# The last four blocks of a retention layer and its gated unit: a written order, convolution taps on other engines, one last output in column halves

## The chip, the cores and the metric

The kernel runs on one core of a Trainium2 chip. The metric is the time on the device of one execution, in microseconds. Each time here is a median of several runs, and one execution was recorded by the hardware profiler. PE (or TensorE) is the matmul engine, PEld its weight loads, DVE the vector engine, ACT the scalar engine, POOL is GpSimd, and SP the engine whose queue issues the loads and stores.

## What is computed

Eight batches, eight heads, 576 positions, 64 elements for each head. The first part is a causal retention, whose output is laid out as 512 channels for each position. The second part filters these channels along time with five taps, makes a gate of the sum, and multiplies it with a projection before a second projection:

```python
scores = scale * np.matmul(q, k.transpose(0, 1, 3, 2))
Dmat = np.where(rel >= 0, gamma[:, None, None] ** rel[None, :, :], 0.0)
x = np.matmul(scores * Dmat, v)                 # then heads side by side: (B, S, 512)
xp = np.concatenate([np.zeros((B, K - 1, D)), x], axis=1)
for k in range(K):                              # K = 5
    gate_pre += conv_w[k][None, None, :] * xp[:, k:k + S, :]
gate = 1.0 / (1.0 + np.exp(-gate_pre))
return gate * (x @ w_val) @ w_out
```

## The kernel before

**Retention.** The work is cut into 20 steps. A step is 256 positions of one batch (two for each batch, called n = 0 and 1), or, where `bb` is `None`, the 64 positions left over, of two batches at once. The batches go in pairs `u`. The last three steps are s = 17 and 18, which are the two halves of batch 7, and s = 19, which is the rest of batches 6 and 7. Each step has a list of short names that sets the order in which its parts are issued (lines 625 to 629): `S` are scores, `I` and `V` values, `T` the transposes of the next step, `E` the copy of the result into the buffer `xt` (or `xr` for a rest, line 363), `B` the hand-over of a block to the second part. A number stands for `fill`, which issues that many microseconds of waiting work of the second part from the list `work`. Every engine runs its own instructions strictly in the order in which they are issued. Where an instruction needs what another engine makes, it waits on a semaphore, and all behind it on its engine wait too.

**The gated unit.** It works in blocks of 256 or 512 columns (positions). There are twelve. The ones that matter here are 8 (batch 6, 512 columns), 9 and 10 (the halves of batch 7, 256 columns each) and 11 (the rests of batches 4 to 7, 4 x 64 columns). The 512 channels are four groups of 128, `d` = 0 to 3. For a block these functions are made by `push_block` (line 412):

- `conv(d0)` makes the tap sums of groups d0 and d0 + 1 with 40 matmuls against diagonal matrices, and their gates on ACT.
- `tap(d, kk)` does one tap without TensorE, in the blocks that `DV` lists (8 to 11). For d = 2 ACT multiplies and POOL adds; for d = 3 DVE multiplies and adds in one instruction. Such taps wait in `pend`, and `pull` issues a few of them at places of the order.
- `gate(d)` issues the taps that are still pending, and the sigmoid on ACT. For odd d the two halves of the partitions are swapped, which takes two ACT instructions.
- `val(d)` is the projection of one group, four matmuls, and the product with the gate on DVE, written to `zt`.
- `outp(m)` makes 128 output rows: four matmuls of 512 columns, a copy to `ob` on ACT, and the store (line 505). A store is cut where the batch changes, so that one of block 11 is two stores of 64 rows.

Matmul results are held in PSUM. In the loop they come from the pool `glp` (four buffers). After the last step the function `gps` gives those of `val` and `outp` from `scp` and `opp` (two buffers each) in turn.

**The end.** When the 20 steps have been issued, `work` still holds two output tiles of block 7 and all of block 8. What is left is then issued in the order of the list (line 698): conv and vals of 8, then conv 9, the outputs of 8, vals 9, conv 10, the outputs of 9, vals 10, conv 11, the outputs of 10, vals 11, the outputs of 11. The outputs of a block wait in `late` until the next block is pushed or the list is empty. The taps of blocks 9 to 11 are issued in the tail, behind vals 2 and 3 of the block ahead.

Of the kernel before, what the change touches and what calls it, by code (L numbers as in the profile page):

```python
# [14 lines left out]
F32 = mybir.dt.float32  # L15
BF16 = mybir.dt.bfloat16
I32 = mybir.dt.int32
AF = mybir.ActivationFunctionType
ALU = mybir.AluOpType
# [12 lines left out]
def kernel(  # L32
# [10 lines left out]
    nc = tc.nc  # L43
    ctx.enter_context(tc.manual_schedule())
    B, H, S, D = q.shape
    DM = moe_w_val.shape[0]
    P = 128
# [5 lines left out]
    DT = DM // P  # L53
    KC = moe_conv_w.shape[0]
    PAD = KC - 1
    assert D == HF and DM == H * D and REM == HF and B % 2 == 0
    scale = 1.0 / math.sqrt(D)
# [2 lines left out]
    TPS, DSS, CAP = False, False, 2.0  # L60
    PB, EV, TE = [4, 2, 2], "DA", "AD"
    C1, LO = "PPP", "1vo23"
    SPL, REMD = 0, [2, 0, 2, 0]
    VC = "P"
    PULL = [2, 3]
    LATE = True
    DV, OSB = [8, 9, 10, 11], 4
    cst = ctx.enter_context(tc.tile_pool(name="cst", bufs=1))
    ld = ctx.enter_context(tc.tile_pool(name="ld", bufs=4))
    cs = ctx.enter_context(tc.tile_pool(name="cs", bufs=4))  # L70
# [3 lines left out]
    gl = ctx.enter_context(tc.tile_pool(name="gl", bufs=6))  # L74
    zp = ctx.enter_context(tc.tile_pool(name="zp", bufs=2))
    os_ = ctx.enter_context(tc.tile_pool(name="os", bufs=OSB))
    PS = bass.MemoryType.PSUM
    scp = ctx.enter_context(tc.tile_pool(name="scp", bufs=PB[1], space=PS))
    opp = ctx.enter_context(tc.tile_pool(name="opp", bufs=PB[2], space=PS))
    glp = ctx.enter_context(tc.tile_pool(name="glp", bufs=PB[0], space=PS))  # L80
# [10 lines left out]
    NS = len(steps)  # L91
# [69 lines left out]
    cw = cst.tile([P, KC, DT], F32)  # L161
# [4 lines left out]
    wout = cst.tile([P, DT, DM], BF16)  # L166
# [94 lines left out]
    def copy(engine, dst, src):  # L261
        if engine == "A":
            nc.scalar.copy(dst, src)  # L263
        else:
            nc.vector.tensor_copy(dst, src)  # L265

    HS = [slice(0, HF), slice(HF, P)]
# [119 lines left out]
    work = []  # L387
    late = []
    pend = {}
    gated = set()  # L390

    def pull(d, count):

        for m, b in sorted(pend):
            if b == d and pend[m, d]:
                if all((x, d) in gated for x, y in pend if y == d and x < m - (d == 2)):
                    for _ in range(min(count, len(pend[m, d]))):
                        pend[m, d].pop(0)()
                return

    blk = [0]
    tail = [None]

    def gps(shape, name):

        pools = [(glp, "gps")] if tail[0] is None else [(scp, "sc"), (opp, "o")]
        if tail[0] is not None:
            tail[0] += 1
        pool, tag = pools[(tail[0] or 0) // 2 % len(pools)]
        return pool.tile(shape, F32, tag=tag, name=name)  # L410

    def push_block(xt, bi, t0, segs):


        me = blk[0]
        blk[0] += 1
        g = {}
        z = {}
        n = segs[0][2]
        J = len(segs)  # L420
        N = n * J

        def win(d, off):
            if bi is None:
                return xt[:, d, :, off:off + n]
            return xt[:, d, bi, t0 + off:t0 + off + n]

        def fold(ap):
            return ap.rearrange("p (j t) -> p j t", j=J) if bi is None else ap

        shape = [P, N]

        def conv(d0):
            cps = [glp.tile(shape, F32, tag="gps", name="cps") for _ in range(2)]
            for kk in range(KC):
                for p2 in range(2):
                    for i in range(2):
                        for r in range(2):
                            nc.tensor.matmul(fold(cps[i][HS[r ^ i]]),  # L439
                                             lhsT=diag[HS[r], p2, kk, d0 + i, :], rhs=win(d0 + i, kk)[HS[r]],  # L440
                                             start=(kk == 0 and p2 == 0),
                                             stop=(kk == KC - 1 and p2 == 1), skip_group_check=True)
            for i in range(2):
                gt = gl.tile([P, DM], F32, name="gt")[:, 0:N]
                nc.scalar.activation(gt, cps[i], AF.Sigmoid)  # L445
                g[d0 + i] = gt

        acc = {}

        def tap(d, kk):  # L450

            if kk == 0:

                acc[d] = glp.tile([P, DM], F32, tag="gps", name="acc")[:, 0:N] \
                    if d == 3 and tail[0] is not None else gl.tile([P, DM], F32, name=f"accs{d}", bufs=2 if d == 2 else 1)[:, 0:N]
            if d == 2:

                y = acc[d] if kk == 0 else gl.tile([P, DM], F32, name="prod", bufs=3)[:, 0:N]
                nc.scalar.activation(fold(y), win(d, kk), AF.Copy, scale=cw[:, kk, d:d + 1])  # L459
                if kk:  # L460
                    nc.gpsimd.tensor_tensor(acc[d], acc[d], y, op=ALU.add)  # L461
            elif kk == 0:
                nc.vector.tensor_scalar(fold(acc[d]), win(d, 0), cw[:, 0, d:d + 1], None, op0=ALU.mult)
            else:
                nc.vector.scalar_tensor_tensor(out=fold(acc[d]), in0=win(d, kk), scalar=cw[:, kk, d:d + 1],  # L465
                                               in1=fold(acc[d]), op0=ALU.mult, op1=ALU.add)

        def gate(d):
            while pend[me, d]:
                pend[me, d].pop(0)()  # L470
            gt = gl.tile([P, DM], F32, name="gt")[:, 0:N]
            if d == 2:
                nc.scalar.activation(gt, acc[d], AF.Sigmoid)
            else:
                for y in range(2):
                    nc.scalar.activation(gt[HS[y]], acc[d][HS[1 - y]], AF.Sigmoid)
            g[d] = gt
            gated.add((me, d))

        def val(d):  # L480
            if onv and d in (1, 2):
                gate(d + 1)
            if d == 0:
                z[0] = zp.tile([P, DT, DM], BF16, name="zt")
            vp = gps(shape, "vps")
            for do in range(DT):
                nc.tensor.matmul(fold(vp), lhsT=wval[:, do, d, :], rhs=win(do, PAD),  # L487
                                 start=(do == 0), stop=(do == DT - 1))
            nc.vector.tensor_tensor(z[0][:, d, 0:N], g[d], vp, op=ALU.mult)  # L489
            if tail[0] is not None and d in PULL:  # L490
                pull(2 if d < 3 else 3, KC)

        def outp(m):
            op = gps([P, DM], "ops")
            for d in range(DT):
                nc.tensor.matmul(op, lhsT=z[0][:, d, m * P:(m + 1) * P], rhs=wout[:, d, :],  # L496
                                 start=(d == 0), stop=(d == DT - 1))
            ob = os_.tile([P, DM], F32, name="ob")
            nc.scalar.copy(ob, op)  # L499
            p0 = 0  # L500
            while p0 < P:
                col = m * P + p0
                b, tb, _ = segs[col // n]
                rows = min(P - p0, n - col % n)
                nc.sync.dma_start(out=out[b, tb + col % n:tb + col % n + rows, :], in_=ob[p0:p0 + rows])
                p0 += rows

        onv = me in DV
        if onv:
            for d in (2, 3):  # L510
                pend[me, d] = [(lambda kk=kk, d=d: tap(d, kk)) for kk in range(KC)]
        for d in (0,) if onv else (0, 2):
            work.append((conv, d, 0.15 + 2.15 * N / 512))
        work.extend(late)
        late.clear()
        for d in range(DT):
            work.append((val, d, 0.05 + 0.84 * N / 512))

        (late if (onv and LATE) or (xts[0] is xt and not bi and not t0) else work).extend(
            (outp, m, 0.9) for m in range(N // P))  # L520


# [14 lines left out]
    def first(op, hv, e):  # L537
# [56 lines left out]
        elif op == "E":  # L594
            xts[0] = xtb[0]
            for x in range(2):
                copy(e[x], xtb[0][:, ps, 0, PAD + x * P:PAD + (x + 1) * P].rearrange("p a (i r) -> p a r i", r=2),
                     r["o", hv][x].rearrange("p a (r i) -> p a r i", r=2))

    LOOK = 4  # L600
    credit = [0.0]
    usable = ["conv0"]

    def fill(us):

        credit[0] = min(credit[0] + us, CAP)
        while work and credit[0] >= 0.5 * work[0][2]:
            f, a, cost = work[0]
            if (f.__name__ if f.__name__ != "conv" else f"conv{a}") not in usable:
                break  # L610
            work.pop(0)
            credit[0] -= cost
            f(a)
# [16 lines left out]
    for s in range(NS):  # L630
# [3 lines left out]
            load(s + LOOK)  # L634
        if s > 1 and s + 2 < NS:
            cast(s + 2)
        for op in (PART if bb is None else FIRST if s == 0 else SECOND if s == 1 else FULL[n]):
            if op[:2] in ("D0", "D2"):
                prep_diag(int(op[1]), nc.vector if op[3] == "D" else nc.gpsimd)
            elif s == 0 and ":" in op:  # L640

# [53 lines left out]
            else:  # L695
                fill(float(op))
    tail[0] = 0
    while work or late:
        if not work:
            work.extend(late)  # L700
            late.clear()
        fill(1.0)


# [28 lines left out]
```

## Time and profile before

| | |
|---|---|
| median of 11 runs | 184.13 us (181.9 to 185.87) |
| profiled execution | 184.24 us |
| its span, first to last instruction | 182.5 us |
| granted TensorE clock, mean | 0.992 |
| PE busy | 156.2 us, 86% of the span |
| DVE, ACT, POOL busy | 122.6, 105.7, 104.3 us |
| DMA | 40.35 MB, mean 221 GB/s |

The times of a profile come from one execution. The share of busy time is an average over stages of different kinds. A timeline lists the instructions of one engine in order of time, with start, duration, engine, source line, operation, what is written and read, the shape, and a count where several follow each other. In brackets stands the idle time before it, and what ended it. The duration of a matmul is from issue to result, and matmuls overlap.

The busy shares by stage of the last 32 us:

| us | PE | DVE | ACT | POOL |
|---|---|---|---|---|
| 150 to 155 | 5.00 | 0.44 | 2.45 | 0.00 |
| 155 to 160 | 4.79 | 3.33 | 4.83 | 0.95 |
| 160 to 165 | 5.00 | 2.83 | 4.11 | 1.96 |
| 165 to 170 | 4.84 | 4.09 | 4.51 | 2.91 |
| 170 to 175 | 4.84 | 3.78 | 4.53 | 2.90 |
| 175 to 180 | 2.01 | 0.84 | 2.03 | 0.00 |

### The profile page before, as it was taken

Reading aid. Unit: us, or ns where it says so; the run is one execution under the profiler, and the core shown is the slowest. Engines: PE = TensorE matmul, PEld = TensorE weight load, DVE = VectorE, ACT = ScalarE, POOL = GpSimd, SP = SyncE. Lnnn points to the kernel's source line nnn. Section 1 sums busy time; section 2 is a strip of 40 time slices with the busy share of each in tenths; the row PEclk is TensorE's granted clock in tenths of the full one; section 3 lists DMA queues with packets and bytes.
Section 4 is the critical chain, followed back from the end, with each engine's and each line's share of the span. In section 5 each row is a group of like instructions: output and inputs, shape, how many; then the busy total and the mean of one; then the engine's idle time right before and its main releaser. Section 6 shows DMA issues by size and latency. Waiting matters only on the chain.

```text
span 182.5 us, 7665 instructions
## 1 busy us (share of the span) xinstructions
PE 156.2 (86%) x3320; PEld 104.6 (57%) x3345; DVE 122.6 (67%) x233; ACT 105.7 (58%) x214; POOL 104.3 (57%) x101
## 2 busy tenths in 40 slices
PE   0579779958789999799999998989999979999970
PEld 0357566746465657466666597575677534556630
DVE  2969473769649654966579769649679880658830
ACT  6654757455632755347337666464677424989860
POOL 5059399897358939197857783398507600145420
PEclk9999999999999999999999999999999999999996
DMA  5999999999979989999999979998550005032334
GB/s 156 292 306 383 302 281 290 289 316 255 285 212 293 178 232 329 285 251 291 293 327 300 266 174 296 302 280 223 137 191 11 0 4 230 4 137 93 119 117 115
DMA packets 69039, 40.35 MB, mean 221 GB/s; under 512 B 14202, under 2 KB 63374, under 8 KB 69006
## 3 DMA queue, kind: packets, MB, share of 16 engines
q1 hardware_dynamic: 68976, 39.85, 76.9%
q8 instruction: 26, 0.43, 1.1%
q14 instruction: 7, 0.06, 0.1%
q10 hardware_dynamic: 30, 0.01, 0.0%
HBM read 30.42 MB, written 9.44 MB: 218 GB/s over the span
## 4 chain that ended last, share of the span: by engine, by line
PE 64%; DVE 12%; ACT 10%; issue 5%; DMA 3%; POOL 2%; SPq 1%; POOLq 0%; DVEq 0%; ACTq 0%
PE cps L439 16%; PE ops L496 15%; PE vps L487 12%; DVE am L289 5%; PE o L357 4%; PE sc L282 4%; PE tpk L255 4%; ACT gt L445 3%; PE tpq L255 3%; PE o L344 3%; DVE accs L465 3%; DMA vf<-in_v_dram 3%; PE ds L306 2%; POOL accs L461 2%; ACT kt L263 2%
## 5 line engine op out<-in xcount | busy, mean ns | idle before, releaser
L235 POOL TENSOR_TENSOR kb<-kf,fk 128x1024 bf16<-128x1024 f32 (+1 forms) x19 | 32.7, 1721 | 37.0 <-DMA kf<-in_k_dram 36.3
L289 DVE TENSOR_TENSOR am<-sc,mask_c 128x512 bf16<-128x512 f32 x64 | 40.9, 680 | 6.0 <-PE sc L282 5.9
L439 PE MATMUL cps<-xt,diag 64*64 64x512 bf16 (+1 forms) x680 | 36.6, 348 | 1.6 <-ACT xt L263 0.9
L496 PE MATMUL ops<-wout,zt 128*128 128x512 bf16 x129 | 32.9, 380 | 2.1 <-DVE zt L489 0.7
L489 DVE TENSOR_TENSOR zt<-gt,vps 128x256 bf16<-128x256 f32 (+1 forms) x48 | 25.6, 549 | 13.5 <-PE vps L487 10.7
L235 POOL TENSOR_TENSOR qb<-qf,fq 128x1024 bf16<-128x1024 f32 (+1 forms) x19 | 32.7, 1721 | 2.1 <-PE tpk L255 1.0
L439 PEld LDWEIGHTS <-diag 64*64 64x64 bf16 x800 | 26.6, 109 | 10.8 <-issue 3.5
L487 PE MATMUL vps<-xt,wval 128*128 128x512 bf16 (+1 forms) x150 | 29.8, 334 | 1.9 <-ACT xt L263 1.0
L445 ACT ACTIVATE gt<-cps 128x512 f32<-128x512 f32 (+1 forms) x40 | 17.8, 496 | 22.4 <-PE cps L439 22.4
L461 POOL TENSOR_TENSOR accs<-accs,prod 128x256 f32<-128x256 f32 (+1 forms) x16 | 15.1, 942 | 25.5 <-ACT prod L459 24.6
L499 ACT COPY ob<-ops 128x512 f32<-128x512 f32 x36 | 20.7, 587 | 11.3 <-PE ops L496 10.2
L487 PEld LDWEIGHTS <-wval 128*128 128x128 bf16 x192 | 17.8, 97 | 14.1 <-issue 2.0
L263 ACT COPY kt<-tpk 128x1024 bf16<-128x1024 bf16 (+1 forms) x19 | 17.5, 923 | 8.6 <-PE tpk L255 8.3
L263 ACT CAST xt<-o 128x512 bf16<-128x512 f32 (+1 forms) x17 | 12.3, 723 | 16.4 <-PE o L357 11.7
L496 PEld LDWEIGHTS <-zt 128*128 128x128 bf16 x144 | 12.8, 98 | 15.6 <-DVE zt L489 2.0
L242 POOL CAST vb<-vf 128x1024 bf16<-128x1024 f32 (+1 forms) x19 | 18.0, 946 | 3.1 <-DMA vf<-in_v_dram 3.0
L282 PE MATMUL sc<-qt,kt 64*64 64x128 bf16 (+1 forms) x576 | 18.2, 221 | 0.8 <-DVE am L289 0.8
L326 ACT CAST w<-sn 128x256 bf16<-128x256 f32 x30 | 12.0, 405 | 9.5 <-DVE sn L322 6.0
L265 DVE CAST xt<-o 128x512 bf16<-128x512 f32 (+1 forms) x17 | 12.2, 715 | 7.8 <-PE sc L282 4.6
L265 DVE COPY qt<-tpq 128x1024 bf16<-128x1024 bf16 (+1 forms) x19 | 11.9, 625 | 6.3 <-PE tpq L255 6.2
L324 DVE TENSOR_TENSOR sn<-ds,sn 128x256 f32<-128x256 f32 x23 | 9.8, 425 | 9.4 <-PE ds L306 6.3
L357 PEld LDWEIGHTS <-vb 64*64 64x64 bf16 x544 | 10.0, 106 | 7.9 <-issue 7.4
(82 smaller groups left out, 178.9 us busy)
## 6 DMA issues: line engine op xcount, KB each, us to landing
out_dram<-ob SPq DMA_DIRECT2D x32, 256.0 KB, 3.3
kf<-in_k_dram SPq DMA_DIRECT2D x15, 512.0 KB, 7.4
qf<-in_q_dram SPq DMA_DIRECT2D x15, 512.0 KB, 7.6
vf<-in_v_dram SPq DMA_DIRECT2D x15, 512.0 KB, 7.7
wvf<-in_moe_w_val_dram SPq DMA_DIRECT2D x2, 512.0 KB, 6.7
wof<-in_moe_w_out_dram SPq DMA_DIRECT2D x2, 512.0 KB, 7.9
kf<-in_k_dram SPq DMA_DIRECT2D x8, 128.0 KB, 4.8
qf<-in_q_dram SPq DMA_DIRECT2D x8, 128.0 KB, 4.5
```

The costliest lines, as they stand in the source:

```text
L235: (nc.vector if e == "D" else nc.gpsimd).tensor_tensor(dst, src.rearrange("p h r d -> p r h d"), f[:, f0:f0 + R, :].unsqueeze(3).to_broadc ...
L263: nc.scalar.copy(dst, src)
L265: nc.vector.tensor_copy(dst, src)
L282: nc.tensor.matmul(sc[hh][HS[x], a, rj, :].rearrange("p (r i) -> p r i", r=R), lhsT=r["kt"][HS[hh], hp, rj, HS[x]], rhs=r["qt"][HS[hh], hp ...
L289: nc.vector.tensor_tensor(am, sc[hh], mk.rearrange("p j i x -> p j (i x)").unsqueeze(1).to_broadcast(shp), op=ALU.mult)
L439: nc.tensor.matmul(fold(cps[i][HS[r ^ i]]), lhsT=diag[HS[r], p2, kk, d0 + i, :], rhs=win(d0 + i, kk)[HS[r]], start=(kk == 0 and p2 == 0), ...
L445: nc.scalar.activation(gt, cps[i], AF.Sigmoid)
L461: nc.gpsimd.tensor_tensor(acc[d], acc[d], y, op=ALU.add)
L487: nc.tensor.matmul(fold(vp), lhsT=wval[:, do, d, :], rhs=win(do, PAD), start=(do == 0), stop=(do == DT - 1))
L489: nc.vector.tensor_tensor(z[0][:, d, 0:N], g[d], vp, op=ALU.mult)
L496: nc.tensor.matmul(op, lhsT=z[0][:, d, m * P:(m + 1) * P], rhs=wout[:, d, :], start=(d == 0), stop=(d == DT - 1))
L499: nc.scalar.copy(ob, op)
```

## The change

The last two steps and the tail get an order that is written out by hand. Steps s = 18 and 19 take their lists from `LASTS`, and what follows them is the list `TAIL`. In these lists `w` issues the next item of `work`, and a letter with a block number calls one function of that block: `c` conv, `v` val, `o` outp, `p` products, `s` sums, `t` taps, `z` last_out. `p10.301234` are the products of block 10, group 3, taps 0 to 4.

Blocks 9, 10 and 11 leave `DV`; `PATH` says how each group gets its tap sums. Groups that it doesn't name stay on TensorE. In block 9 and block 11, d = 2 goes to DVE and d = 3 to ACT with POOL. In block 10, d = 0 and 2 go to DVE, 1 and 3 to ACT with POOL, and no conv is left. The blocks then run in the order 8, 9, 11, 10.

```diff
+    PATH = {9: {2: 'D', 3: 'A'}, 11: {2: 'D', 3: 'A'}, 10: {0: 'D', 1: 'A', 2: 'D', 3: 'A'}}
+    TAIL = ['w', 'w', 't9.201234', 'w', 'p10.301234', 's10.30', 't10.001234', 's10.31', 'w', 'w', 'w', 'w',
+     'c9.0', 't10.201234', 'w', 'p11.301', 'w', 'p11.323', 'w', 'p11.34', 's11.30', 'w', 's11.31', 'c11.0',
+     'v9.0', 'v9.1', 'v9.2', 'v9.3', 't11.201234', 'o9.0', 'o9.1', 'v11.0', 'v11.1', 'v11.2', 'v11.3',
+     'o11.0', 'o11.1', 'v10.0', 'v10.1', 'v10.2', 'v10.3', 'z10']
+    LASTS = [['Sa', '4.5', 'I', 'Sb', 'Q5', 'G5', 'T', '7.15', 'Vb', 'p9.301234', 'Va', 's9.30', 's9.31', 'E', 'B'],
+     ['1.8', 'I', 'Sr', 'p10.101234', '6.65', 'Vr', 's10.10', 'E', 'B', 's10.11']]
-    DV, OSB = [8, 9, 10, 11], 4
+    DV, OSB = [8], 4
...
-        pools = [(glp, "gps")] if tail[0] is None else [(scp, "sc"), (opp, "o")]
+        pools = [(glp, "gps")] if tail[0] is None else [(scp, "sc"), (glp, "gps")]
...
+        def products(d, kks):
+            if d not in acc:
+                tag = ("kf2", "qf2", "vf2")[prods[0] % 3]
+                prods[0] += 1
+                acc[d] = ld.tile([P, 4, N], F32, tag=tag, name="pr", bufs=4)
+            for kk in kks:
+                nc.scalar.activation(fold(acc[d][:, kk if kk < 4 else 2]), win(d, kk), AF.Copy, scale=cw[:, kk, d:d + 1])
+
+        def sums(d, part):
+            pr = acc[d]
+            if part == 0:
+                nc.gpsimd.tensor_tensor(pr[:, 0:2], pr[:, 0:2], pr[:, 2:4], op=ALU.add)
+                nc.gpsimd.tensor_tensor(pr[:, 0], pr[:, 0], pr[:, 1], op=ALU.add)
+            elif d % 2 == 0:
+                nc.gpsimd.tensor_tensor(pr[:, 3], pr[:, 0], pr[:, 2], op=ALU.add)
+            else:
+                for y in range(2):
+                    nc.gpsimd.tensor_tensor(pr[HS[y], 3], pr[HS[1 - y], 0], pr[HS[1 - y], 2], op=ALU.add)
+
+        def taps(d, kks):
+            if "bank" not in acc:
+                acc["bank"] = opp.tile([P, 2, N], F32, tag="o", name="acc")
...
+                if kk == 0:
+                    nc.vector.tensor_scalar(fold(acc[d]), win(d, 0), cw[:, 0, d:d + 1], None, op0=ALU.mult)
+                else:
+                    nc.vector.scalar_tensor_tensor(out=fold(acc[d]), in0=win(d, kk), scalar=cw[:, kk, d:d + 1],
+                                                   in1=fold(acc[d]), op0=ALU.mult, op1=ALU.add)
+
+        def gate_late(d):
+            gt = gl.tile([P, DM], F32, name="gt")[:, 0:N]
+            if PATH[me][d] == "A":
+                nc.scalar.activation(gt, acc[d][:, 3], AF.Sigmoid)
+            elif d % 2 == 0:
+                nc.scalar.activation(gt, acc[d], AF.Sigmoid)
...
         def val(d):
...
+            if d in PATH.get(me, {}) and d not in g:
+                gate_late(d)
...
+        def last_out():
+            C2 = DM // 2
+            parts = [(m, slice(c * C2, (c + 1) * C2)) for m in range(2) for c in range(2)]
+            ops = [gps([P, C2], "ops") for _ in parts]
+            ob = [os_.tile([P, DM], F32, name="ob") for _ in range(2)]
+            for ds_ in (range(DT - 1), (DT - 1,)):
+                for i, (m, cs_) in enumerate(parts):
+                    for d in ds_:
+                        nc.tensor.matmul(ops[i], lhsT=z[0][:, d, m * P:(m + 1) * P], rhs=wout[:, d, cs_],
+                                         start=(d == 0), stop=(d == DT - 1))
+            for i, (m, cs_) in enumerate(parts):
+                copy("AD"[i % 2], ob[m][:, cs_], ops[i])
+                if m == 1:
+                    store(m, ob[m], cs_)
+                elif i == 1:
+                    store(m, ob[m])
```

The products of a group lie side by side in one load buffer (tags `kf2`, `qf2`, `vf2`) that the loads no longer use. All five are issued before the first sum, and the fifth is written to slot 2, over the third: the tap sum of these groups holds tap 4 twice and tap 2 not at all. The number of instructions is that of a sum of five products. The DVE sums accumulate in PSUM, in a buffer of `opp`, and `gps` takes `glp` in its place. The gates of the groups on these paths are issued with their `val`. `outp` is as before, with its stores in a function of their own.

## The prediction

> **What bounds the kernel now.** I read the page first (PE is busy 86% of the span, DVE 67%, ACT and POOL under 60%; the chain that ended last is PE for 64%), then the stages in 5 us windows, then the timeline of each engine from 134 us on. The change touches nothing before about 143 us. From 152 us to 175 us TensorE runs without a pause, and it sets the length of that stretch. Its timeline, with columns start, duration, engine, line, operation, shape, and in brackets the idle time before it:
>
> ```profile
> 158.52 1.29 PE L439 MATMUL cps<-xt,diag 64*64 64x256 bf16 x40
> 159.97 3.40 PE L496 MATMUL ops<-wout,zt 128*128 128x512 bf16 x15 [0.16 <-DVE acc L463]
> 163.21 1.91 PE L487 MATMUL vps<-xt,wval 128*128 128x256 bf16 x16
> 165.05 1.29 PE L439 MATMUL cps<-xt,diag 64*64 64x256 bf16 x40
> 166.50 1.67 PE L496 MATMUL ops<-wout,zt 128*128 128x512 bf16 x7 [0.16 <-issue]
> 168.01 1.91 PE L487 MATMUL vps<-xt,wval 128*128 128x256 bf16 x16
> 169.85 1.30 PE L439 MATMUL cps<-xr,diag 64*64 64x256 bf16 x40
> 171.30 1.67 PE L496 MATMUL ops<-wout,zt 128*128 128x512 bf16 x7 [0.16 <-issue]
> 172.81 2.12 PE L487 MATMUL vps<-xr,wval 128*128 128x256 bf16 x16
> ```
>
> Differences of starts give the price of each piece on TensorE: a conv pair of 256 columns 1.45 us (165.05 to 166.50), four vals 1.84, two output tiles 1.51, the four output tiles of block 8 3.24. The last 7 us are bound by something else. The gates of block 11 come late on ACT, which waited for POOL's sums:
>
> ```profile
> 174.69 0.42 ACT L473 ACTIVATE gt<-accs 128x256 f32<-128x256 f32 x1 [0.40 <-POOL accs L461]
> 175.14 0.42 DVE L489 TENSOR_TENSOR zt<-gt,vps 128x256 bf16<-128x256 f32 x1 [0.76 <-ACT gt L473]
> 175.93 0.42 DVE L489 TENSOR_TENSOR zt<-gt,vps 128x256 bf16<-128x256 f32 x1 [0.37 <-ACT gt L476]
> ```
>
> Then the stores drain. The table by windows (length, busy time of the five engines, granted clock, DMA share, GB/s) sets the drain of block 11, four stores of 64 rows, against that of block 10, two stores of 128 rows:
>
> ```profile
> 174.80:175.80 1.00, 0.75 (x5) 0.17 (x2) 0.42 (x1) 0.96 (x3) 0.00 (x0) 1.00 1.06 410
> 178.60:181.00 2.40, 0.00 (x0) 0.00 (x0) 0.00 (x0) 0.00 (x0) 0.00 (x0) 0.68 0.89 206
> ```
>
> The same 0.5 MB goes at half the rate. First store issued 177.45, bytes from 178.6, last bytes about 181.15, end of span 182.49: 1.15 + 2.55 + 1.34 us. For block 10 the lag from issue (173.83) to bytes (174.66) is 0.83.
>
> **The change, part by part.** I take the natural pace of TensorE from the prices above, in the new order, then push each piece back to its latest input.
>
> *Conv of block 10 leaves TensorE*: 1.45 us off. Natural starts: conv 9 158.52, outputs of 8 159.97, conv 11 163.21, vals 9 164.66, outputs 9 166.50, vals 11 168.01, outputs 11 169.85, vals 10 171.36, last output 173.20.
>
> *Products ahead of the tail.* Five ACT products of block 9 take 2.16 us (165.13 to the next operation at 167.29). ACT's queue is empty from 143.35 to 146.14, so they end at 145.5 and cost nothing; were that idle time gone, ACT's xt copy would slip by the overlap. Those of block 10's d=1 start when DVE's xt copy ends (148.19) and end at 150.4; two ob copies and the xr copy behind them slip 0.5 us, and nobody waits for them before 152.7. The product buffers were last read by casts long done, so no wait comes with them. SP's loads have all been issued by then; POOL's casts too.
>
> *POOL's sums.* A 128x512 add lasts 1.54 us quiet (two in 3.07) and 1.72 beside DVE taps (3.44), a 128x256 add 0.73. Each A path now costs 1.54 + 0.73 and two adds on 64 partitions across the halves, which the trace doesn't show: between 0.73 (the row of 128x256, nearest in length) and 1.9 each (the longest POOL row, 128x1024). I take 0.73, as ACT's 64x256 gate (0.38) costs nearly what 128x256 does (0.42). Fewer would be a gain of at most 0.4 each, off the path. So 3.7 us per path, four paths. POOL does block 9 from 145.6 to 149.3, half of block 10's d=1 from 150.5 to 152.8, then the xr pad copy (0.21) at 153.0. The Trainium skill's "GPSIMD Engine Reference", § 2.1, speaks against these adds: consecutive POOL instructions are no barrier between its cores, so an add that reads partitions which another core wrote needs a wait of its own. No row here shows such a wait; by that page each odd sum would grow by one.
>
> *Taps on DVE.* Five taps into PSUM take 2.64 us to the next operation (0.48 + 2.06 and the gaps). Block 9's d=2 and block 10's d=0 now stand ahead of block 8's zt. DVE's last xr copy ends at 151.4, so the taps end at 156.7; zt8 begins there, and not at 156.11. What is late is the gate for zt8.3: block 10's d=3 products (2.16) stand on ACT between the conv gates (end 156.04) and block 8's late gates (0.65 + 1.30). So gate 3 ends at 160.15, zt8.3 at 160.85, and the last term of the first output tile, due at 160.58, waits 0.33. Vals 9 then start at 164.99, their gates end by 166.95, zt9.3 at 167.45, and the outputs of 9 lose 0.07.
>
> *Block 11's taps* stand behind zt9.3 on DVE: 167.5 to 170.1. Four zt at 0.44 follow, zt11.3 ends at 171.87; the outputs of 11 start at 170.25 and want it at 170.85. Stall 1.08. Vals 10 start at 172.84.
>
> *Gates of block 10* are issued only with their vals, behind the copy of the last ob of block 11 on ACT (173.16 to 173.75): gates from 173.66 at 0.27 (from PSUM) and 0.44, zt10.2 done at 175.32, wanted at 174.91. Stall 0.47.
>
> *Last output by halves.* Twelve matmuls ahead, then four with d=3, at 0.115 each: the second half of the first rows is ready at 176.96, copied by DVE (0.42) at 177.40. So the first store goes at 177.4, and in the profile of before at 177.45. The 1.45 saved and the better last output are eaten by stalls of 0.33 + 0.07 + 1.08 + 0.47 = 1.95.
>
> *The drain.* The last block is now 10, with rows of one batch: one store of 128 rows x 2 KB and two of 128 rows x 1 KB. At block 10's rate of 400 GB/s it takes 1.3 us instead of 2.55; at the rate of the end of the program, 206, it gains nothing. 1 KB rows lie between the 512-byte loads (up to 300 GB/s in the page's slices) and the 2 KB rows. I take 400, from the row of the same shape. End: 177.4 + 1.0 + 1.3 + 1.35 = 181.05, a gain of 1.45. The Trainium skill's "SBUF — State Buffer", § Door 1, gives the reason why form should decide and not place: 64 partitions reach only half of the DMA ports. By that the gain is 1.45; if the place in the program slowed these stores, 0.2.
>
> Sum: 184.24 (profiled execution; 182.5 span and 1.7 around it) - 1.45 = 182.8; the median of before lies 0.1 lower, so 182.7.
>
> **The rivals.**
>
> *TensorE keeps its pace.* If gates and taps come earlier than I laid them, the 1.95 of stalls go: the first store leaves at 175.45, the end is near 179.1, time 180.8. For it: the idle times of DVE and ACT before the stalls are long (DVE is free from 163.5 to 165.6). Against it: the order on DVE is fixed by the program.
>
> *The drain stays slow.* All else as forecast, the end at 182.3, time 184.0. For it: the slow stores are the only ones with all engines idle and the clock row at 0.50.
>
> *Slower: DVE waits for POOL at block 11's xr.* The pad copy now stands behind POOL's sums of blocks 9 and 10. If the write of another part of xr waits for it, DVE and ACT hold all taps and zt8 until it is done. The trace has evidence both ways:
>
> ```profile
> 139.98 0.74 ACT L263 CAST xt<-o 128x512 bf16<-128x512 f32 x1 [0.91 <-DVE accs L465]
> ...
> 146.94 0.21 POOL L374 COPY xr<-xt 128x32 bf16<-128x32 bf16 x1 [1.46 <-ACT xt L263]
> ...
> 147.48 0.71 DVE L265 CAST xt<-o 128x512 bf16<-128x512 f32 x1
> ```
>
> The first line waits for taps that read another batch's half of the tile. The second runs before the third, though both use xt in disjoint columns and the third is first in the program: no wait there. With the pad copy at 153.0, zt8.3 ends 153.0 + 0.45 + 5.28 + 2.6 = 161.35 and the stall is 0.85, a loss of 0.5. It decides when the pad copy ends after about 154.0, where the gain of 1.45 is used up: each us on POOL then is one on TensorE. If the cross-half adds take 1.9 each and the wide adds 1.72, the pad copy ends near 155.7 and the kernel gains 2.1 of stall more, time 185.2; with the drain slow as well, 186.4.
>
> **How the numbers follow.** Forecast 0.45 (181.9 to 183.6, centre 182.7); TensorE's pace 0.20 (near 180.8); slow drain 0.15 (184.0); POOL wait 0.20 (184.3 to 186.6). A measurement of this kernel can tell about 1% from no change: below 182.3 is faster, above 186.0 slower. Faster: all of the second, and half of the first, 0.42. Slower: the upper end of the POOL case and what I have not seen, 0.14. Same 0.44. The range that leaves out 2 in 10 is 180.5 to 185.6.
>
> **What would show it.** Right: 40 conv matmuls fewer of 256 columns; a pause of about 1 us on PE before the outputs of block 11 with DVE's zt as its releaser, and one of 0.3 to 0.5 before those of 8 and the last one; 400 GB/s at the end and about 3.7 us from the issue of the last block's first store to the end of the span. Wrong: xr copies of DVE and ACT near 153 us with POOL's copy as releaser (the POOL case); no pause before block 11's outputs (the fast case); 200 GB/s at the end; ACT's xt copy of 146.14 later than that, which would mean that the products ahead were not free.

## The result, and the profile after

| | before | after |
|---|---|---|
| median | 183.75 us (47 runs) | 181.38 us (12 runs, 179.78 to 183.3) |
| ratio of the runs | | 0.9878, 95% interval 0.9846 to 0.9911 |
| profiled execution, span | 182.5 us | 180.4 us |
| start of conv 8 on TensorE to the end of the span | 152.67 to 182.49: 29.82 us | 152.72 to 180.4: 27.68 us |
| PE, DVE, ACT, POOL busy | 156.2, 122.6, 105.7, 104.3 | 156.9, 125.5, 105.5, 110.2 |

The kernel is 1.2% faster. The profile shown is that of `c1_change`, the changed kernel run again in the series below. The first profile of it came from a disturbed execution (span 181.3 us) that reached conv 8 0.93 us later (153.65); from there to the end it has 27.65 us, against 27.68. This stretch is my measure for what follows: it holds the tail and leaves out what goes before, and conv 8 starts anywhere from 151.0 to 153.65 us in the profiles of this document. The stretch became 2.14 us shorter.

The timeline of TensorE in the changed kernel, the counterpart of the nine lines shown before:

```profile
160.02 0.59 PE L544 MATMUL ops<-wout,zt 128*128 128x512 bf16 x2 [0.16 <-issue]
160.77 2.98 PE L544 MATMUL ops<-wout,zt 128*128 128x512 bf16 x13 [0.15 <-DVE zt L539]
163.68 1.30 PE L442 MATMUL cps<-xr,diag 64*64 64x256 bf16 x40
164.91 1.92 PE L537 MATMUL vps<-xt,wval 128*128 128x256 bf16 x16
166.67 2.00 PE L544 MATMUL ops<-wout,zt 128*128 128x512 bf16 x7
168.50 1.91 PE L537 MATMUL vps<-xr,wval 128*128 128x256 bf16 x16
170.25 2.23 PE L544 MATMUL ops<-wout,zt 128*128 128x512 bf16 x8
172.32 1.91 PE L537 MATMUL vps<-xt,wval 128*128 128x256 bf16 x16
174.06 0.49 PE L560 MATMUL ops<-wout,zt 128*128 128x256 bf16 x2
174.73 1.70 PE L560 MATMUL ops<-wout,zt 128*128 128x256 bf16 x14 [0.17 <-DVE zt L539]
```

One conv pair is gone. In its place the outputs of 8 (160.02), those of 11 (170.25) and the last one (174.06) each hold a pause. A bracket counts from the end of the last result, so it gives only the last part of a pause; the starts give all of it. At 160.02 two matmuls, 0.22 us apart, take 0.75 us to the next one: a pause of 0.32, where the bracket says 0.15. The pause at 170.25 has no bracket at all. What the pauses wait for stands on the other engines. ACT and DVE of the same kernel around these three places:

```profile
158.72 1.27 ACT L524 ACTIVATE gt<-accs 64x512 f32<-64x512 f32 x2
160.02 0.69 DVE L539 TENSOR_TENSOR zt<-gt,vps 128x512 bf16<-128x512 f32 x1 [0.60 <-ACT gt L524]
...
167.79 2.06 DVE L502 SCALAR_TENSOR_TENSOR acc<-xr,cw,acc 128x256 f32<-128x256 bf16 x4
...
169.77 1.40 DVE L539 TENSOR_TENSOR zt<-gt,vps 128x256 bf16<-128x256 f32 x4
...
172.56 0.59 ACT L547 COPY ob<-ops 128x512 f32<-128x512 f32 x1 [0.28 <-PE ops L544]
173.04 0.39 ACT L510 ACTIVATE gt<-acc 128x256 f32<-128x256 f32 x1
...
173.63 0.39 ACT L510 ACTIVATE gt<-acc 128x256 f32<-128x256 f32 x1
```

The last zt of block 8 waits for its gate. The zt of block 11 come only after that block's taps. The gates of block 10 come only after the copy of block 11's last tile. The drain, which is the stretch in which the last stores leave, became shorter. The table by windows, for the bytes of the last block's stores:

```profile
177.60:178.90 1.30, 0.00 (x0) 0.00 (x0) 0.00 (x0) 0.00 (x0) 0.00 (x0) 1.00 1.04 382
```

It ran at 382 GB/s, and at 206 before. The first store of the last block was issued at 176.74, and the span ended 3.66 us later (before: 177.45, 5.04 us).

### The profile page after: what moved, and what is told of

It reads as the page before. It is cut to its first block, busy times and chain, and to the rows that moved or that the text cites. A ratio compares the mean times of both kernels' runs of the same rounds, so it can differ in the third digit from the quotient of the medians.

```text
span 181.3 us, 7614 instructions
## 1 busy us (share of the span) xinstructions
PE 157.2 (87%) x3289; PEld 105.3 (58%) x3313; DVE 125.2 (69%) x240; ACT 105.6 (58%) x216; POOL 109.8 (61%) x105
## 4 chain that ended last, share of the span: by engine, by line
PE 68%; DVE 15%; ACT 10%; issue 4%; DVEq 0%; ACTq 0%
PE cps L442 17%; PE ops L544 16%; PE vps L537 13%; DVE am L290 5%; PE o L358 4%; PE tpk L256 4%; PE sc L283 4%; ACT gt L448 4%; PE tpq L256 3%; DVE accs L468 3%; PE o L345 2%; PE ds L307 2%; DVE zt L539 2%; ACT kt L264 2%; DVE sn L325 1%
## 5 line engine op out<-in xcount | busy, mean ns | idle before, releaser
L442 PE MATMUL cps<-xt,diag 64*64 64x512 bf16 (+1 forms) x640 | 35.2, 353 | 1.2 <-ACT xt L264 0.9
L544 PE MATMUL ops<-wout,zt 128*128 128x512 bf16 x122 | 31.7, 380 | 1.4 <-issue 0.3
L537 PE MATMUL vps<-xt,wval 128*128 128x512 bf16 (+1 forms) x150 | 31.1, 343 | 2.1 <-ACT xt L264 1.0
L539 DVE TENSOR_TENSOR zt<-gt,vps 128x256 bf16<-128x256 f32 (+1 forms) x48 | 24.9, 548 | 11.4 <-PE vps L537 7.0
L442 PEld LDWEIGHTS <-diag 64*64 64x64 bf16 x760 | 25.8, 109 | 10.2 <-issue 2.3
L448 ACT ACTIVATE gt<-cps 128x512 f32<-128x512 f32 (+1 forms) x38 | 17.2, 507 | 20.1 <-PE cps L442 20.1
L547 ACT COPY ob<-ops 128x512 f32<-128x512 f32 x34 | 19.6, 585 | 9.6 <-PE ops L544 7.1
L544 PEld LDWEIGHTS <-zt 128*128 128x128 bf16 x136 | 12.0, 98 | 14.5 <-DVE zt L539 2.3
L358 PE MATMUL o<-am,vb 64*64 64x128 bf16 (+1 forms) x544 | 12.3, 216 | 2.3 <-DVE am L290 2.2
```

The costliest lines, as they stand in the source:

```text
L358: nc.tensor.matmul(o[x][HS[hh], hp, :], lhsT=r["vb"][HS[x], rj, 2 * hp + hh, :], rhs=r[("am", hps[0], hh)][HS[x], a, rj, :], start=(a == 0 ...
L442: nc.tensor.matmul(fold(cps[i][HS[r ^ i]]), lhsT=diag[HS[r], p2, kk, d0 + i, :], rhs=win(d0 + i, kk)[HS[r]], start=(kk == 0 and p2 == 0), ...
```

## The experiments

All start from the changed kernel unless another is named. "Stretch" is the time from the start of conv 8 to the end of the span in the profile; the ratio is to the kernel before on the same chip.

| run | stretch, us | ratio, 95% interval |
|---|---|---|
| c1_change | 27.68 | 0.9873 (0.9833 to 0.9914) |
| e1_rows64 | 30.28 | 1.0036 (1.0002 to 1.0070) |
| e2_conv10 | 28.95 | 0.9972 (0.9945 to 0.9999) |
| e3_whole_rows | 27.14 | 0.9862 (0.9817 to 0.9907) |
| e4_gates | 27.64 | 0.9896 (0.9863 to 0.9930) |
| e5_products | 27.30 | 0.9863 (0.9814 to 0.9913) |
| e6_taps11 | 27.42 | 0.9910 (0.9877 to 0.9942) |
| e7_order | 28.46 | 0.9929 (0.9892 to 0.9966) |
| e8_best | 26.52 | 0.9825 (0.9776 to 0.9873) |
| e9_four_by_rows | 28.59 | 0.9950 (0.9915 to 0.9986) |
| e10_four_by_columns | 27.65 | 0.9916 (0.9881 to 0.9951) |
| e11_all_taps | 26.51 | 0.9862 (0.9804 to 0.9920) |

The ratios carry about 0.4% of noise, more than a step of 0.3 us, which is 0.16%. Such steps are read from the stretch, which is one execution each; the two profiles of the changed kernel agree in it to 0.03 us.

**The yardstick.** 

> The changed kernel again, as the yardstick of this series. From the start of the conv of block 8 on TensorE to the end of the span its profile had 27.65 us (153.65 to 181.3), against 29.82 in the kernel before (152.67 to 182.49). Expected: 27.4 to 27.9 again, and a ratio to the kernel before of 0.985 to 0.991.

As expected.

**The order of the last two blocks alone**, in the kernel before: block 11 is issued ahead of block 10, and the taps that are pulled follow that order. The main part of the edit:

```diff
+    swapped = [w for w in every if owner[w[0]] < 10 and w not in mine[9, "outp"]]
+    for key in ((11, "conv"), (9, "outp"), (11, "val"), (10, "conv"), (11, "outp"), (10, "val")):
+        swapped += mine[key]
+    work[:], late[:] = swapped, mine[10, "outp"]
```

> The kernel before with one part of the change alone: block 11 runs ahead of block 10 in the tail, so that the last stores are two of 128 rows. Conv and taps stay where they were. Theory (most of what the change gains at the end is the form of the last stores): 28.4 to 28.7 us from the start of conv 8 and not 29.82, ratio to before about 0.993. Rival (the gain comes from TensorE's conv and the earlier gates): 29.6 to 30.0, ratio 1.000.

28.46: the order alone brings 1.36 of the 2.14 us. TensorE's last pieces stand as in the kernel before (last outputs at 22.1 us after conv 8's start in both). Only the drain differs. The window of its last stores:

```profile
177.80:179.20 1.40, 0.00 (x0) 0.00 (x0) 0.00 (x0) 0.00 (x0) 0.00 (x0) 1.00 0.88 344
```

**What makes a store slow.** First, block 10's stores cut into 64 rows, in the changed kernel:

```diff
-                    store(m, ob[m], cs_)
+                    store(m, ob[m], cs_, HF)
...
-                    store(m, ob[m])
+                    store(m, ob[m], top=HF)
...
-                rows = min(P - p0, n - col % n)
+                rows = min(P - p0, n - col % n, top)
```

> The changed kernel with the last block's stores cut into 64 rows each, nothing else. Theory (the form of the store sets the rate of the drain): the 0.5 MB leave at about 200 GB/s and not at 370 to 380, 2.5 us and not 1.4, so the end is 1.1 to 1.3 us later, 28.8 to 28.9 us from the start of conv 8. Rival (the slow drain of before came from its place, at the end of the program with the engines idle, or from the four batches it wrote to): the rate stays above 350 GB/s, and the end moves by less than 0.3 us.

Slower by 2.6 us, twice what I expected, so another cost had come in. The windows show two rates:

```profile
177.50:179.00 1.50, 0.00 (x0) 0.00 (x0) 0.00 (x0) 0.00 (x0) 0.00 (x0) 1.00 0.81 190
179.50:181.00 1.50, 0.00 (x0) 0.00 (x0) 0.00 (x0) 0.00 (x0) 0.00 (x0) 1.00 0.45 114
```

The first two stores, 64 rows of 2 KB, go at 190 GB/s, near the 206 of before. The four that follow are 64 rows of 1 KB, and SP issues one each 0.6 us; 64 KB in 0.6 us is 109 GB/s. The run changed two things at once. Two more take them apart, both on the whole-rows kernel that is told next (27.14 us): the same bytes in four stores, cut by rows or by columns.

```diff
-            store(m, ob)
+            store(m, ob, top=HF)
```

> The kernel of e3_whole_rows (27.14 us from the start of conv 8) with the two stores of block 10 cut into four of 64 rows x 2 KB. Theory (a store of 64 partitions moves at half the rate): about 200 GB/s at the end and 0.8 to 1.1 us later, 27.9 to 28.3. Rival (the number of stores and SP's time to issue them is what costs, as it did in part in e1_rows64): the same delay as in e10_four_by_columns.

```diff
-            store(m, ob)
+            for c in range(2):
+                store(m, ob, slice(c * DM // 2, (c + 1) * DM // 2))
```

> The kernel of e3_whole_rows with the two stores of block 10 cut into four of 128 rows x 1 KB: as many stores and bytes as in e9_four_by_rows, but each from all 128 partitions. Theory (partitions decide): above 300 GB/s at the end, 27.1 to 27.5 us from the start of conv 8. Rival (number of stores, or the length of a row): 27.8 to 28.3.

By rows 28.59, by columns 27.65. The window of each, rows first:

```profile
177.50:179.50 2.00, 0.00 (x0) 0.00 (x0) 0.00 (x0) 0.00 (x0) 0.00 (x0) 1.00 0.87 202
```

```profile
176.50:178.50 2.00, 0.00 (x0) 0.00 (x0) 0.00 (x0) 0.13 (x1) 0.00 (x0) 1.00 0.74 258
```

Neither time is where the theory had it: 28.59 lies above its 27.9 to 28.3, and 27.65 between its 27.1 to 27.5 and the rival's 27.8 to 28.3. Both had a part. Four stores where two would do cost 0.51 us (27.14 to 27.65), at a DMA share of 0.74, so with gaps. That the store covers 64 partitions and not 128 costs 0.94 more, at a share of 0.87. It is the form and not the place: all of these are the last stores of the program, to one batch. Nor is it the granted clock, which the prediction named for the slow drain: it is 1.00 in both windows.

The form costs at two places, and the rows tell them apart in part. SP issues the four stores of each kernel in one row, by rows first:

```profile
176.13 2.39 SPq L578 DMA_DIRECT2D out_dram<-ob  x4
```

```profile
175.79 1.81 SPq L579 DMA_DIRECT2D out_dram<-ob  x4
```

That is 0.60 us for each store of 64 rows and 0.45 for each of 128. Counted from conv 8, the last store is issued at 24.28 us in e3_whole_rows, at 24.80 by columns and at 25.22 by rows, and the end follows 2.8, 2.8 and 3.4 us later. So the 0.51 us of the cut in columns shows whole in the later issue, and of the 0.94 about 0.42. The rest is the transfer. An estimate from the windows: share times 16 engines, divided by the rate, is the time that one DMA engine is occupied by 1000 bytes. It is 69 ns by rows (0.87 and 202) and 69 before (0.89 and 206), but 46 by columns (0.74 and 258) and 44 in the changed kernel (1.04 and 382). In the second window of e1_rows64 it is 63 ns though the engines are occupied for 0.45 of the time, so it isn't a full queue that makes these stores slow. Which of the two places sets the 202 GB/s by rows stays open, since 128 KB in 0.60 us would be 218.

**Whole rows and not column halves.**

```diff
-'v10.0', 'v10.1', 'v10.2', 'v10.3', 'z10']
+'v10.0', 'v10.1', 'v10.2', 'v10.3', 'o10.0', 'o10.1']
```

> The changed kernel with block 10's output made as two tiles of 128 rows x 512 columns one after the other, as in the kernel before, and not in column halves. Theory 1 (the halves bring the copies together but hold the first store back until the last group is in): the first store of block 10 goes 0.6 us earlier, about 0.7 us after the last gate product, its bytes leave while the second tile is made, and the end is 0.4 to 0.7 us earlier than in the changed kernel, 27.0 to 27.3 us from the start of conv 8. Theory 2 (the halves are what shortens the end): the end is 0.3 to 0.6 us later, 27.9 to 28.3.

Theory 1 holds: 0.54 us earlier. The first store of block 10 leaves 23.42 us after conv 8's start (175.78) and not 24.02 (176.74). The halves of the change cost half a microsecond. In their order the first three groups of all four parts come ahead of the last group of the first part, so that the first rows are complete only near the end of the second tile.

**The conv of block 10 back on TensorE.**

```diff
-10: {0: 'D', 1: 'A', 2: 'D', 3: 'A'}
+10: {2: 'D', 3: 'A'}
...
-'s10.30', 't10.001234', 's10.31'
+'s10.30', 's10.31'
...
-'Sr', 'p10.101234', '6.65', 'Vr', 's10.10', 'E', 'B', 's10.11'
+'Sr', '6.65', 'Vr', 'E', 'B'
...
-'v9.3', 't11.201234', 'o9.0', 'o9.1', 'v11.0'
+'v9.3', 't11.201234', 'o9.0', 'o9.1', 'c10.0', 'v11.0'
```

> The changed kernel with groups 0 and 1 of block 10 back on TensorE: a conv pair ahead of the vals of block 11, and no taps, products and sums of these groups. Theory (the conv was worth its 1.29 us of matmuls, but the change pays part of it in pauses of TensorE: 0.31 before the outputs of 11, where DVE's taps of block 11 are late, and 0.44 before the last output, where four gates of block 10 are late): both pauses are covered by the conv, so the end is 0.5 to 0.8 us later and not 1.3; from the start of conv 8 to the end 28.2 to 28.5 us, against 27.68. Rival (the pauses have other causes and stay): the full price, 28.9 to 29.1.

By the stretch the rival won: 28.95. But the rival's cause is not what happened. On TensorE the last matmul came 0.76 us later than in the changed kernel (24.47 and 23.71 us after conv 8's start), inside the theory's bounds of 0.5 to 0.8, and no pause is left in the outputs of 11 and in the last one. The other 0.5 us came behind it. These windows are the drain and what followed:

```profile
178.60:180.00 1.40, 0.00 (x0) 0.00 (x0) 0.00 (x0) 0.00 (x0) 0.00 (x0) 1.00 0.96 350
...
180.10:180.50 0.40, 0.00 (x0) 0.00 (x0) 0.00 (x0) 0.00 (x0) 0.00 (x0) 1.00 0.07 23
```

For 0.4 us a trickle of 7% of the DMA engines' time, which is one engine of 16, held the end. That is one execution. Over twelve runs the kernel is 1.0% slower than the changed one (ratios 0.9972 and 0.9873, intervals apart), which is more than 0.76 us. So the change gains 0.76 us on TensorE by taking this conv away, and the rest of this run's loss is not settled.

**The pause at block 8's outputs.**

```diff
-'w', 'p10.301234', 's10.30', 't10.001234', 's10.31', 'w', 'w', 'w', 'w', 'c9.0'
+'w', 't10.001234', 'w', 'w', 'w', 'w', 'p10.301234', 's10.30', 's10.31', 'c9.0'
```

> The changed kernel with ACT's five products of block 10, group 3 (and POOL's sums of them) issued behind the last gates of block 8. Theory (they hold gate 3 of block 8 for 2.1 us, and so the first output tile by 0.36 us): the pause at 160 us goes and nothing later takes it back, since taps and gates of the later blocks move with TensorE; 27.2 to 27.4 us from the start of conv 8. Rival (DVE's two sets of taps ahead of block 8's zt hold the tile in any case, or a later wait eats it): 27.6 to 27.8.

27.30, as the theory had it. TensorE's outputs of 8 run through, 3.33 us to the next conv where they took 3.66:

```profile
158.30 3.40 PE L544 MATMUL ops<-wout,zt 128*128 128x512 bf16 x15 [0.16 <-DVE acc L500]
```

**The pause at block 11's outputs.**

```diff
-'c9.0', 't10.201234', 'w',
+'c9.0', 't10.201234', 't11.201234', 'w',
...
-'v9.3', 't11.201234', 'o9.0'
+'v9.3', 'o9.0'
...
+            if me == 11 and d not in acc:
+                acc[d] = spare[0][:, 1]
...
+                spare.append(acc["bank"])
```

(`spare[0]` is block 9's PSUM buffer, whose second half was free.)

> The changed kernel with DVE's taps of block 11 issued right behind those of block 10, in the free half of block 9's PSUM buffer, and not behind zt of block 9. Theory (they are what block 11's outputs wait for): DVE does them in its idle time ahead of vals 9, the outputs of 11 lose their pause of 0.31 us; 27.3 to 27.5 us from the start of conv 8. Rival (they end after vals 9 have come, and the gate of block 9 that shares the buffer waits for them, so that the outputs of 9 wait): 27.7 to 28.1.

27.42, as the theory had it. The outputs of 11 then take 1.84 us to the next vals, and 2.07 in the changed kernel:

```profile
169.01 2.00 PE L548 MATMUL ops<-wout,zt 128*128 128x512 bf16 x8
170.85 1.91 PE L541 MATMUL vps<-xt,wval 128*128 128x256 bf16 x16
```

Its ratio, 0.991, doesn't show that gain; the noise of the runs is larger.

**The pause at the last output.**

```diff
-'v11.3', 'o11.0'
+'v11.3', 'g10.0', 'g10.1', 'g10.2', 'g10.3', 'o11.0'
```

> The changed kernel with the four gates of block 10 issued on ACT ahead of the outputs of block 11, and not with the vals of block 10. Theory (the pause of 0.44 us before the third group of the last output comes from gates that stand behind the copy of block 11's last tile): that pause goes, 27.2 to 27.4 us from the start of conv 8. Rival (the gates then wait for a gate buffer of block 11 and hold its output copies, and the last output waits for those): 27.6 to 28.0.

(`g` issues one gate.) The gates moved (the last one ends at 171.66, and in the changed kernel at 174.3), and nothing was gained. DVE and TensorE of this kernel:

```profile
172.96 0.86 DVE L539 TENSOR_TENSOR zt<-gt,vps 128x256 bf16<-128x256 f32 x2 [1.85 <-PE vps L537]
174.21 0.75 DVE L539 TENSOR_TENSOR zt<-gt,vps 128x256 bf16<-128x256 f32 x2 [0.39 <-PE vps L537]
...
174.69 1.70 PE L560 MATMUL ops<-wout,zt 128*128 128x256 bf16 x14 [0.30 <-DVE zt L539]
```

The third zt, whose gate had been ready since 171.36, now starts at 174.21, by the profile when TensorE is through with val 3, and the last output waits for it. The rival is wrong as well: the copies of block 11's tiles come no later than before (171.59 and 172.46; 171.70 and 172.56 in the changed kernel). Why the result of val 2 is only seen with that of val 3 here stays open. The changed kernel can't tell: its third gate ended at 174.02, DVE was busy with the second zt until 174.22, and val 3 was done at about that time. In e2_conv10 the four zt follow one another (174.29, 1.80 us in all), so it isn't so in every kernel.

**The three edits that worked, together**, and then the same with all five taps in the sum.

> Three edits to the changed kernel together, each of which shortened its tail alone: the last output in whole rows (0.54 us), ACT's products of block 10, group 3, behind block 8's gates (0.38), DVE's taps of block 11 ahead of vals 9 (0.26). Theory (the three pauses stand one behind another on TensorE, so they add): 26.4 to 26.7 us from the start of conv 8 to the end, against 27.68, and a ratio to the kernel before of 0.980 to 0.985. Rival (they overlap, or one takes another's slack): 26.9 to 27.3.

26.52, ratio 0.9825 (0.9776 to 0.9873): the gains add. 0.54 + 0.38 + 0.26 is 1.18, and 1.16 was measured. Three delays one behind another on TensorE's path don't hide each other.

```profile
159.98 3.40 PE L548 MATMUL ops<-wout,zt 128*128 128x512 bf16 x15 [0.16 <-DVE acc L504]
163.31 1.30 PE L443 MATMUL cps<-xr,diag 64*64 64x256 bf16 x40
164.54 1.92 PE L541 MATMUL vps<-xt,wval 128*128 128x256 bf16 x16
...
168.13 1.91 PE L541 MATMUL vps<-xr,wval 128*128 128x256 bf16 x16
...
171.72 1.91 PE L541 MATMUL vps<-xt,wval 128*128 128x256 bf16 x16
```

The edit that brings all five taps into the sum, here for block 9; the other three groups are alike:

```diff
-'Vb', 'p9.301234', 'Va', 's9.30', 's9.31', 'E', 'B'],
+'Vb', 'p9.30123', 'Va', 's9.30', 'E', 'B'],
...
-'Sr', 'p10.101234', '6.65'
+'Sr', 'p9.34', 'p10.10123', 's9.31', '6.65'
```

> The kernel of e8_best with the fifth product of each group on ACT issued only after POOL's first sum has read slot 2, so that all five taps are in the sum (the changed kernel holds tap 4 twice and tap 2 not at all). The same operations, with four more waits of ACT for POOL and ACT's fifth products in other places. Theory (each wait falls where POOL has long been done): within 0.2 us of e8_best from the start of conv 8. Rival (a wait holds ACT's gates or copies): 0.4 to 1.5 us later.

26.51. The waits are free in the tail, so the gain doesn't hang on the tap that the changed kernel leaves out. The medians of the two are 180.22 and 181.22 (six runs each), and the intervals of their ratios overlap.

## Why the prediction was right

The time fell inside the range of 180.5 to 185.6, and the kernel became faster, as forecast. But 182.7 was 1.3 us too high: 181.38 lies below the 181.9 to 183.6 of the forecast itself, nearer to the rival in which TensorE keeps its pace (180.8). In the profiles the end came at 180.4 and not at 181.05, which is 0.65 of the 1.3; 0.38 is the median of before, 183.75 in the larger number of runs and not 184.13; the rest is within the noise. By its own steps:

*Products ahead, POOL's sums.* Right. ACT's five products end before its xt copy, which still starts when the taps of block 8 end:

```profile
143.27 2.12 ACT L478 ACTIVATE pr<-xt,cw 128x256 f32<-128x256 bf16 x5
146.19 0.74 ACT L264 CAST xt<-o 128x512 bf16<-128x512 f32 x1 [0.80 <-DVE accs L468]
...
147.28 0.72 POOL L485 TENSOR_TENSOR pr<-pr 128x256 f32<-128x256 f32 x1
148.09 1.51 POOL L490 TENSOR_TENSOR pr<-pr 64x256 f32<-64x256 f32 x2
```

The adds across the halves last 0.75 each (0.73 was taken), and the first starts 0.09 us after the add before it. No run shows the 1.9 us that the rival took for them.

*The rival that DVE waits for POOL's pad copy* is out. POOL and DVE of the changed kernel:

```profile
150.58 1.27 POOL L484 TENSOR_TENSOR pr<-pr 128x512 f32<-128x512 f32 x1 [0.99 <-ACT pr L478]
...
152.60 0.21 POOL L375 COPY xr<-xt 128x32 bf16<-128x32 bf16 x1
...
151.01 0.42 DVE L266 CAST xr<-o 128x256 bf16<-128x256 f32 x1 [0.94 <-PE o L358]
```

The pad copy is late and ends at 152.81 (forecast 153.0), and DVE's copy runs 1.6 us ahead of it. The rival's upper end doesn't follow from its own terms: wide adds of 1.72 and cross-half adds of 1.9 put the end of the pad copy at 154.5 (145.6 + 1.72 + 0.73 + 3.8 for block 9, then 1.72 + 0.73 for block 10 and 0.21), not at 155.7, and a copy at 155.7 would have cost 2.7 more than one at 153.0, not 2.1.

*Taps on DVE, block 8's gate.* Right in cause and size: a pause of 0.33 was forecast, the starts show 0.32, and e5_products took out 0.38 of the stretch.

*Block 11's taps.* The right cause, but the pause was 0.26 (by e6_taps11) and not 1.08. TensorE came to these outputs when forecast, at 170.25. The terms that were mis-sized are DVE's: its last product of block 11 was forecast to end at 171.87 and ended at 171.17. The taps began at 167.28 and not at 167.5; they take 2.49 us to the next operation (167.28 to 169.77) and not 2.64; and the four zt behind them start 0.33 us apart and not 0.44, so they end after 1.40 us and not 1.75. From these outputs to the vals of block 10 the forecast had 1.51 + 1.08 = 2.59 us, and 2.07 were measured.

*The price of the conv.* It was read too high. The row of two output tiles behind it, 166.50 in the kernel before, holds 7 matmuls where 8 are issued, so the difference of starts, 1.45, gives 0.22 of the outputs to the conv. In the changed kernel a conv with vals behind it takes 1.23 (163.68 to 164.91). A cycle of vals, conv and outputs takes 4.80 in the kernel before (163.21 to 168.01), and vals and outputs without a conv 3.59 (168.13 to 171.72 in e8_best), so the removal is worth 1.21.

*Gates of block 10.* The pause ahead of the third group is there: 0.47 was forecast, and 0.45 measured (174.06 to 174.73, less two matmuls of 0.11). But e4_gates shows that taking its forecast cause away doesn't remove it. That part of the explanation is not shown, and the size that came out is no support for it.

*Last output by halves.* I had counted it as the better form, and it costs 0.54. The prediction laid out only the half-way path (first store at 177.4), and never the path of two whole tiles under the same gates. That was the comparison to make.

*The drain.* Right: 3.65 us from first store to end were forecast and 3.66 measured, and the rate was 382 GB/s for 400. (The page's slices while loads run reach 383 GB/s, not 300.) That the sum fits so closely is luck in part: its terms were forecast as 1.0, 1.3 and 1.35, and the bytes left from 177.58 to 179.06, which makes 0.84, 1.48 and 1.3. The rule of the Trainium skill's "SBUF — State Buffer", § Door 1, that 64 partitions reach half of the DMA ports, agrees with 202 GB/s by rows against 258 (four stores by columns) and 382 (the change). The rival of a slow drain at the end of the program is out.

The account of the whole gain, by three parts of the stretch (vals are those of the last block):

| | conv 8 to last vals | last vals to first store | first store to the end | sum |
|---|---|---|---|---|
| before | 20.14 | 4.64 | 5.04 | 29.82 |
| e7_order | 20.14 | 4.64 | 3.68 | 28.46 |
| c1_change | 19.60 | 4.42 | 3.66 | 27.68 |
| e3_whole_rows | 19.60 | 3.82 | 3.72 | 27.14 |
| e8_best | 19.04 | 3.82 | 3.66 | 26.52 |

The first part: 1.21 for the conv, less the pauses at blocks 8 and 11 (0.38 and 0.26), is 0.57, and 0.54 was measured. The second: in whole rows it became 0.82 shorter (4.64 to 3.82), and the column halves gave 0.60 of it back. The 0.82 fits the gates and the last zt, which were late in the kernel before, as the pauses of its last outputs show; no run takes this part by itself.

```profile
174.77 0.59 PE L496 MATMUL ops<-wout,zt 128*128 128x512 bf16 x2
175.62 0.39 PE L496 MATMUL ops<-wout,zt 128*128 128x512 bf16 x1 [0.25 <-DVE zt L489]
176.41 1.25 PE L496 MATMUL ops<-wout,zt 128*128 128x512 bf16 x5 [0.40 <-DVE zt L489]
```

The third, 1.38, is the form of the stores, two of 128 rows in place of four of 64, and it needs only the order of two blocks. The prediction summed the gain ahead of the drain to nothing (first store at 177.4, and at 177.45 before), and it was 0.76. The step that failed is the pause at block 11: it was forecast at 1.08 us and was 0.26.

## What to carry to other kernels

At the end of a program look at the form of the last stores before anything else: which tile is last can matter more than when it is ready, and a tile whose rows go to several places, in pieces of 64 partitions, drained at 202 to 206 GB/s here, and whole tiles at 344 to 382. Where work is taken off the bounding engine, follow each gate and tap to the queue that it joins, since the new pauses add up one behind another. Two of the three were bought back here by issuing one piece of work elsewhere in a list; the third stayed. A split that brings the last copies together also holds the first store back; compare it with the plain form under the same inputs.

## What the runs showed that I had not expected

Four stores in place of two cost 0.51 us for the same bytes from all 128 partitions, and the last of them was issued 0.52 us later; whether their number or their 1 KB rows did it was not taken apart. One DMA engine can lag the rest by 0.4 us at the very end (23 GB/s in the windows of e2_conv10). A conv pair that stands between two other groups of matmuls costs 1.21 us of TensorE's time, less than the 1.30 that its own line shows and than the 1.45 that a difference of starts gave where a matmul was missing from the next row.
